# Attention into balanced experts: loads paced six in front instead of three, x held in pieces and written behind all loads, the gate's norms taken sooner

## The chip, the cores and the metric

One core of a Trainium2 chip runs the whole program. The metric is the device time of one execution in microseconds; lower is better. The kernel before takes 627.1 us, the median of three runs (626.71 to 636.63).

The core has five engines with queues of their own: TensorE (PE; its weight loads are listed as PEld), VectorE (DVE), ScalarE (ACT), GpSimd (POOL) and SyncE (SP), which here does little else than issue transfers. An engine works through its queue in order, and an instruction that waits holds up all that stands behind it.

## The reference

```
kv  = einsum('bhsd,bhse->bhde', k, v)          # 8 batches, 8 heads, 576 rows, 64 columns
out = einsum('bhsd,bhde->bhse', q, kv)
x   = out / sqrt(mean(out*out, -1) + 1e-6) * g_norm   # then (b, h, s, d) -> (b*s, h*d) = 4608 x 512

logits = x @ w_gate                            # 4608 x 8
order  = argsort(-logits.flatten())            # greedy: the largest logit first,
                                               # an expert takes 576 tokens and is then full
for e in range(8):
    y[mask_e] = relu(x[mask_e] @ w1[e]) @ w2[e]
```

There is no softmax: attention is two matrix products and a norm over each head. Which token goes to which expert depends on all logits at once, so the choice can begin only when the last batch's logits are there.

## The kernel before

The program has two parts. The first, attention, is written by hand for TensorE, VectorE, ScalarE and SyncE: on these engines the order in the queue is the order in the code. It fills the logits (lg) and writes the normed rows x to DRAM (x_dram). The second chooses the tokens of one expert after another, gathers their rows out of x_dram with indirect transfers of GpSimd (L793), and runs the experts' two layers on TensorE. Its code is untouched by the change.

**Loads.** k, v and q of a batch come in two halves each, six transfers of 576 KB (load, L83). They are all issued by SyncE, in the order k, v, q, k, v, q, each through paced (L75). The loads of batches 0 and 1 stand at the head of the program, those of batch b+2 at the end of prepare(b) (L401), which runs in pieces inside the work of batch b-1. Each of k, v and q has two buffers, so a load of batch b+2 also waits until TensorE has read batch b. paced adds a wait: from the seventh transfer on, a transfer is issued when the third in front of it in the list has landed. The writes of x go through paced too and are in the same list.

**One batch.** prepare(b) sums k times v over the rows into kv_ps (sum_kv, L341, four pairs of heads, each of 72 or 36 listed matmuls with its neighbour), turns q in five groups (turn_q, L326, against the identity matrix ident), and makes kvx, the right side of the second product: kv itself and, beside it, kv times the gate's weights (gw), so that the second product yields the row and its gate logits at once. work(b) then does four or five tiles of 128 rows (tiles, L410): the product into o_ps (L433), squares on ScalarE, their sum on VectorE, a copy into o_sb. At a batch's end come the norm (inv), the logits (L465), and the scaled rows xo: on GpSimd (L470) for batches 0 to 6, on ScalarE (L475) for the last one. The pieces of prepare(b+1) are slipped between the tiles of work(b), so on TensorE sums and turns of one batch alternate with the products of the batch before.

**Writes of x.** tiles appends to a list of writes, one for each two tiles (512 KB, or 256 KB for a fifth tile alone). At the end of a batch's work, L520 issues writes from the front of the list as long as eight or more wait, and all in the last batch. So the first three writes are issued at the end of the work of batch 3, between the loads of batches 6 and 7. One tile xo of five buffers holds the scaled rows of a batch until they are written.

**The start.** While the first loads come, TensorE runs filler products (ones, L265). The gate's weights and g_norm are loaded by ScalarE's queue (L100, L105). gate_norms (L272) multiplies them, squares and sums them on VectorE, and sums over the partitions on TensorE (L278); from this gate_bound makes the limits between which the later search for thresholds runs. VectorE makes ident out of two iotas (L111 to L117).

## Time and profile before

| | |
|---|---|
| three runs | 627.1, 636.63, 626.71 us |
| the profiled execution | 627.37 us, its span 625.6 us |
| PE busy | 585.3 us, 94% of the span |
| DVE, ACT, POOL busy | 373.3, 179.3, 412.3 us |
| mean granted clock of TensorE | 0.967 |
| read and written in DRAM | 71.32 MB, 18.87 MB |
| loads of k, v, q | 48 of 576 KB |
| writes of x | 16 of 512 KB, 4 of 256 KB |
| first product of batch 7 | 108.73 us |
| gather of the first expert's tokens | from 137.49 us |

The profile is of one execution, whose own time stands in the table; its span runs from the first to the last instruction. Times in its views count from the span's start. The attention lies between 0 and about 118 us; the first choice of tokens, a chain of short steps, between there and 137 us; the experts' layers after that. In the rows, "<-" names what ended a wait, "issue" stands where the profile shows nothing that was waited for, and "x72" is a count of instructions. The clock is the share of full speed that TensorE was granted.

### The profile page before, as it was taken

Reading aid. Unit: us, or ns where it says so; the run is one execution under the profiler, and the core shown is the slowest. Engines: PE = TensorE matmul, PEld = TensorE weight load, DVE = VectorE, ACT = ScalarE, POOL = GpSimd, SP = SyncE. Lnnn points to the kernel's source line nnn. Section 1 sums busy time; section 2 is a strip of 40 time slices with the busy share of each in tenths; the row PEclk is TensorE's granted clock in tenths of the full one; section 3 lists DMA queues with packets and bytes.
Section 4 is the critical chain, followed back from the end, with each engine's and each line's share of the span. In section 5 each row is a group of like instructions: output and inputs, shape, how many; then the busy total and the mean of one; then the engine's idle time right before and its main releaser. Section 6 shows DMA issues by size and latency. Waiting matters only on the chain.

```text
span 625.6 us, 12011 instructions
## 1 busy us (share of the span) xinstructions
PE 585.3 (94%) x4644; PEld 460.5 (74%) x4644; DVE 373.3 (60%) x1172; ACT 179.3 (29%) x387; POOL 412.3 (66%) x367
## 2 busy tenths in 40 slices
PE   7998888459999999999999999999999999999993
PEld 4887777336788678777867886788678877867881
DVE  2676764868878796778728763885481255024320
ACT  1565654814221222022212221221123123213200
POOL 0154434216999989696869668966987796966603
PEclk9999997759999999999999999999999999999997
DMA  8998899748045280092056106503633062010002
GB/s 286 314 312 275 283 305 341 271 137 260 0 143 203 75 318 27 2 344 76 1 178 204 40 16 226 180 1 100 223 98 135 2 210 77 1 51 25 1 2 80
DMA packets 41410, 91.07 MB, mean 146 GB/s; under 512 B 3456, under 2 KB 3456, under 8 KB 41344
## 3 DMA queue, kind: packets, MB, share of 16 engines
q1 hardware_dynamic: 34752, 71.31, 33.5%
q0 software_dynamic: 5888, 18.88, 9.2%
q8 instruction: 39, 0.64, 0.4%
q14 instruction: 27, 0.22, 0.1%
q10 hardware_dynamic: 704, 0.02, 0.1%
HBM read 71.32 MB, written 18.87 MB: 144 GB/s over the span
## 4 chain that ended last, share of the span: by engine, by line
PE 76%; DMA 13%; DVE 5%; issue 2%; POOL 2%; ACT 1%; POOLq 0%; DVEq 0%; ACTq 0%
PE h_ps L966 33%; PE y_ps L1066 31%; DMA v_sb<-in_v_dram 11%; PE y_ps L1080 4%; PE t_ps L874 3%; PE o_ps L433 2%; PE kv_ps L345 1%; DMA q_sb<-in_q_dram 1%; PE given_ps L580 1%; DMA g_col<-in_g_norm_dram 1%; PE given_ps L576 1%; PE qt_ps L330 1%; DVE ms L447 1%; DMA xg<-x_dram,ids 1%; POOL out_dram L883 1%
## 5 line engine op out<-in xcount | busy, mean ns | idle before, releaser
L966 PE MATMUL h_ps<-xt,w_sb 128*128 128x288 f32 x384 | 101.0, 412 | 0.9 <-ACT xt L877 0.8
L978 ACT ACTIVATE hid<-hid 128x288 f32<-128x288 f32 x128 | 55.6, 443 | 147.5 <-DVE hid L961 139.4
L966 PEld LDWEIGHTS h_ps<-xt,w_sb 128*128 128x128 f32 x384 | 70.8, 190 | 24.8 <-issue 5.7
L961 DVE TENSOR_TENSOR hid<-h_ps,u 128x288 f32<-128x288 f32 x128 | 56.8, 454 | 28.9 <-PE h_ps L966 24.6
L966 PE MATMUL h_ps<-sx,sw 128*128 128x288 f32 x256 | 67.9, 407 | 0.1
L793 POOL DMA_INDIRECT xg<-x_dram,ids x40 | 38.2, 955 | 34.9 <-DVE upper L633 22.6
L1066 PE MATMUL y_ps<-tw,sh 128*128 128x256 f32 x256 | 61.1, 383 | 0.0
L1066 PE MATMUL y_ps<-tw,hid 128*128 128x256 f32 x256 | 60.9, 381 | 0.0
L1066 PE MATMUL y_ps<-w_sb,hid 128*128 128x256 f32 x256 | 59.5, 382 | 0.0
L966 PEld LDWEIGHTS h_ps<-sx,sw 128*128 128x128 f32 x256 | 48.4, 190 | 13.9 <-DVE u L961 0.6
L877 ACT ACTIVATE xt<-t_ps,g_col 128x512 f32<-128x512 f32 (+1 forms) x40 | 25.8, 644 | 110.3 <-PE t_ps L874 110.3
L1066 PEld LDWEIGHTS y_ps<-w_sb,hid 128*128 128x128 f32 x256 | 47.4, 190 | 6.4
L1066 PEld LDWEIGHTS y_ps<-tw,sh 128*128 128x128 f32 x256 | 47.3, 190 | 6.1
L1066 PEld LDWEIGHTS y_ps<-tw,hid 128*128 128x128 f32 x256 | 47.1, 190 | 6.0
L470 POOL TENSOR_TENSOR xo<-o_sb,inv 128x512 f32<-128x512 f32 x31 | 32.5, 1077 | 27.7 <-ACT sq L439 11.1
L961 DVE TENSOR_TENSOR y_sb<-y_ps,u 128x512 f32<-128x512 f32 x24 | 16.5, 689 | 53.5 <-PE y_ps L1066 53.5
L961 DVE TENSOR_TENSOR u<-h_ps,u 128x288 f32<-128x288 f32 x96 | 41.9, 449 | 10.3 <-PE h_ps L966 8.3
L433 PE MATMUL o_ps<-kvx,qt 64*128 64x72 f32 (+1 forms) x640 | 41.3, 274 | 4.5 <-DVE kvx L396 2.7
L433 PEld LDWEIGHTS o_ps<-kvx,qt 64*128 64x128 f32 (+1 forms) x640 | 36.3, 182 | 9.1 <-issue 7.8
L896 POOL TENSOR_TENSOR sh<-hid 128x512 f32<-128x512 f32 x16 | 20.3, 1268 | 33.0 <-ACT hid L978 31.9
L896 POOL TENSOR_TENSOR tw<-w_sb 128x512 f32<-128x512 f32 x32 | 40.0, 1272 | 0.2
L883 POOL DMA_INDIRECT out_dram<-y_sb,outs x32 | 31.3, 977 | 11.5 <-issue 10.2
(214 smaller groups left out, 1064.2 us busy)
## 6 DMA issues: line engine op xcount, KB each, us to landing
w_sb<-in_moe_w_dram SPq DMA_DIRECT2D x16, 1024.0 KB, 6.2
w_sb<-in_moe_w_dram SPq DMA_DIRECT2D x8, 2048.0 KB, 14.1
k_sb<-in_k_dram SPq DMA_DIRECT2D x16, 576.0 KB, 5.8
v_sb<-in_v_dram SPq DMA_DIRECT2D x16, 576.0 KB, 6.0
q_sb<-in_q_dram SPq DMA_DIRECT2D x16, 576.0 KB, 6.1
x_dram<-xo SPq DMA_DIRECT2D x16, 512.0 KB, 4.3
x_dram<-xo SPq DMA_DIRECT2D x4, 256.0 KB, 4.7
xg<-x_dram,ids POOLq DMA_INDIRECT x40
```

Of the source, the lines that this page charges most:

```text
L433: nc.tensor.matmul(o_ps[rows_at, rp, (2 * r2 + l) * W:(2 * r2 + l + 1) * W], lhsT=turned_q[bn][ks, l, block // 2:block // 2 + m].rearrange ...
L470: nc.gpsimd.tensor_tensor(xo[:, t], o_sb[:, t, :, 0:D], inv[:, t * H:(t + 1) * H].rearrange("p (h o) -> p h o", o=1).to_broadcast([P, H, D ...
L793: tokens = nc.gpsimd.indirect_dma_start(out=xg[0:nr], out_offset=None, in_=x_dram, in_offset=bass.IndirectOffsetOnAxis(ap=ids[0:nr, n:n + ...
L874: nc.tensor.transpose(t_ps[:, d, 0:nr], xg[0:nr, d * P:(d + 1) * P], ident[0:nr, 0:nr])
L877: nc.scalar.mul(xt[:, :, a:a + nr], t_ps[:, :, 0:nr], g_col)
L883: put = nc.gpsimd.indirect_dma_start(out=out, out_offset=bass.IndirectOffsetOnAxis(ap=ids_of[t][0:nr, n:n + 1], axis=0), in_=y_sb[0:nr, :] ...
L896: in_order(nc.gpsimd.tensor_tensor(o, x, y, op=op))
L961: nc.vector.tensor_tensor(o, p_ps, u, op=AL.add)
L966: nc.tensor.matmul(o, lhsT=left[:, d, f * P:(f + 1) * P], rhs=right[:, d], start=d == 0, stop=d == KH - 1)
L978: nc.scalar.activation(h, h, ACT.Relu)
L1066: nc.tensor.matmul(p_ps[:, n], lhsT=left[:, f, n * P:(n + 1) * P], rhs=right[:, f], start=(f == 0), stop=(f == FH - 1))
L1080: nc.tensor.matmul(y_ps[l * nr:(l + 1) * nr], lhsT=hid[:, l * FH + f, a:a + nr], rhs=w2[:, l * FH + f, :], start=(f == 0), stop=(f == FH - 1))
```

## The change

Four edits in the attention part.

- paced: the wait is for the sixth transfer in front, not the third. It still begins with the seventh transfer.
- The scaled rows are held in pieces of two tiles (12 buffers) or one tile (4 buffers) in place of one tile for a whole batch in five buffers. No write is issued before the end of the work of batch 4, where the list holds twelve; the later ones go at the end of each batch's work. Since the loads of batch 7 are issued within the work of batch 4, all writes stand behind all loads.
- odd, kv, kvt and part have one buffer in place of two.
- gate_norms is called ahead of turn_q(0) and turn_q(1) in prepare(0).

```diff
     loaded = {}
-    AHEAD = 3
+    AHEAD = 6
     issued = []
     def paced(dma):
-        if len(issued) >= 2 * AHEAD:
+        if len(issued) >= AHEAD:
             tc.add_manual_dep(dma.ins, issued[-AHEAD].name,
...
             ones(3)
+            gate_norms()
             turn_q(0)
             turn_q(1)
-            gate_norms()
             ones(4)
...
-        odd = att.tile([D, 2, NP * D], FT, name="odd", tag="odd")
+        odd = att.tile([D, 2, NP * D], FT, name="odd", tag="odd", bufs=1)
...
-        xo = att.tile([P, T, H, D], FT, name="xo", tag="xo", bufs=LAG + 1)
+        xo = [att.tile([P, min(2, T - x), H, D], FT, name="xo", tag=f"xo{min(2, T - x)}", bufs=(4, 12)[min(1, T - x - 1)])
+              for x in range(0, T, 2)]
...
-                nc.gpsimd.tensor_tensor(xo[:, t], o_sb[:, t, :, 0:D],
+                nc.gpsimd.tensor_tensor(xo[t // 2][:, t % 2], o_sb[:, t, :, 0:D],
...
-                xo[:, x:y].rearrange("p t h d -> p t (h d)"))))
+                xo[x // 2].rearrange("p t h d -> p t (h d)"))))
...
-            while len(writes) >= 2 * LAG or b + 1 == B and writes:
+            while b + 4 >= B and writes:
                 writes.pop(0)()
```

kv, kvt and part get bufs=1 in the same way as odd. Three places show how the change moves instructions. SyncE's queue, from the loads of the second half of batch 6 to the first writes, before the change:

```order
L89 DMA q_sb<-in_q_dram 128x2x576
L479 DMA x_dram<-xo 128x2x512 x3
L89 DMA k_sb<-in_k_dram 128x2x576
L89 DMA v_sb<-in_v_dram 128x2x576
L89 DMA q_sb<-in_q_dram 128x2x576
```

and after it, from the second half of batch 7 on:

```order
L89 DMA k_sb<-in_k_dram 128x2x576
L89 DMA v_sb<-in_v_dram 128x2x576
L89 DMA q_sb<-in_q_dram 128x2x576
L479 DMA x_dram<-xo 128x2x512 x4
L479 DMA x_dram<-xo 128x512
L479 DMA x_dram<-xo 128x2x512 x4
```

The three writes that stood between two batches' loads have moved behind the last load.

VectorE's queue at the head of the program, the difference (+ is after, - is before). gone and who are cleared there, row_f is the iota as a number, and qt is the first copy of turned q:

```order
 L214 MEMSET gone 128x36
 L216 MEMSET who 128x36
+L274 TENSOR_SCALAR gw<-gw,g_col 128x64
+L276 TENSOR_TENSOR gsq<-gw 128x64
+L277 TENSOR_REDUCE g_146<-gsq 128x8
 L111 CAST iota_p<-iota_p_i 128x1
 L115 CAST row_f<-row_i 128x128
@@ -29,7 +32,4 @@
 L174 TENSOR_SCALAR know<-iota_p 128x1
 L334 COPY qt<-qt_ps 128x2x256
-L274 TENSOR_SCALAR gw<-gw,g_col 128x64
-L276 TENSOR_TENSOR gsq<-gw 128x64
-L277 TENSOR_REDUCE g_146<-gsq 128x8
```

The three steps on the gate's weights have moved not only ahead of the copy of q but ahead of the two casts from which ident is made.

TensorE's queue at the same place; begun_ps is the target of the fillers and of the gate's sum:

```order
 L268 LDWEIGHTS ones_b
 L268 MATMUL begun_ps<-wide,ones_b 128x512
+L278 MATMUL begun_ps<-g_146,ones_f 128x8
 L330 MATMUL qt_ps<-ident,q_sb 128x128 x8
-L278 MATMUL begun_ps<-g_146,ones_f 128x8
 L268 LDWEIGHTS ones_b
```

The gate's sum has moved ahead of the eight turns of q.

## The prediction

> **What bounds the kernel now.** I read the page first: the span, the clock line, and the chain that ended last.

> ```profile
> span 625.6 us, 12011 instructions
> PEclk9999997759999999999999999999999999999997
> DMA  8998899748045280092056106503633062010002
> PE 76%; DMA 13%; DVE 5%; issue 2%; POOL 2%; ACT 1%; POOLq 0%; DVEq 0%; ACTq 0%
> ```

> The expert layers (from about 146 us on) are PE's own. The DMA share of the chain lies in the first six or seven slices, the attention, and that is where the change lies. So the second view is that stretch cut into pieces of equal work: each row below runs over two batches, from the first o_ps product of batch 1, 3, 5 to that of batch 3, 5, 7. Columns are microseconds, busy time of each engine with its instruction count, granted clock, DMA share, GB/s.

> ```profile
> 30.29:53.21 22.92, 21.91 (x525) 19.13 (x525) 17.02 (x43) 15.12 (x32) 11.87 (x13) 1.00 0.95 310
> 53.21:78.77 25.56, 22.13 (x525) 19.20 (x525) 17.14 (x45) 14.98 (x31) 11.88 (x13) 1.00 0.87 274
> 78.77:108.73 29.96, 26.07 (x525) 22.63 (x525) 17.60 (x44) 15.30 (x32) 11.83 (x13) 0.83 0.93 321
> ```

> The same 525 matmuls take 22.92, then 25.56, then 29.96 us. The first pair is what PE can do when fed: 21.91 of 22.92 us busy. The others are 2.64 and 7.04 us longer, 9.68 us together. That is all that attention can give back without doing less work. What it is made of, the waits of PE between 14 and 109 us show (total, times, longest):

> ```profile
> PE kv_ps L345 <- DMA v_sb<-in_v_dram: 3.0, 3, 1.2
> PE o_ps L433 <- DVE kvx L396: 2.7, 6, 0.8
> PE o_ps L433 <- issue: 1.5, 1, 1.5
> PE qt_ps L330 <- DMA q_sb<-in_q_dram: 0.9, 2, 0.7
> PE qt_ps L330 <- issue: 0.4, 1, 0.4
> ```

> Late loads: 3.0 + 0.9 = 3.9 us. Waits with no releaser ("issue"): 1.5 + 0.4 = 1.9 us. The kvx waits are in the undisturbed pair too, and stay. The remaining 9.68 - 3.9 - 1.9 = 3.9 us is the clock: the third pair has 0.83, and its PE busy time is 26.07 - 21.91 = 4.2 us above the first's, which agrees. The timeline says where these fall.

> ```profile
> 90.33 0.47 PE L433 MATMUL o_ps<-kvx,qt 64*64 64x72 f32 x12 [1.51 <-issue]
> 92.48 1.74 PE L433 MATMUL o_ps<-kvx,qt 64*128 64x72 f32 x16 [0.31 <-DVE kvx L396]
> 95.29 1.33 PE L345 MATMUL kv_ps<-v_sb,k_sb 64*64 64x64 f32 x36 [1.06 <-DMA v_sb<-in_v_dram]
> 97.27 1.09 PE L330 MATMUL qt_ps<-ident,q_sb 128*128 128x128 f32 x4 [0.66 <-DMA q_sb<-in_q_dram]
> ```

> and, in windows of 1 us (columns as above):

> ```profile
> 92.00:93.00 1.00, 0.69 (x10) 0.55 (x9) 0.34 (x2) 1.00 (x4) 0.00 (x0) 0.89 0.91 286
> 93.00:94.00 1.00, 1.00 (x12) 1.00 (x10) 0.75 (x3) 0.08 (x1) 0.00 (x0) 0.50 0.82 187
> ```

> The clock halves late in the 92-93 window, in the middle of a thin stretch: 1.51 us idle before 90.33, 1.06 before 95.29, 0.66 before 97.27.

> **The change part by part.** *Pacing and order of the loads.* Before, a load waits until the third in front has landed, and three writes of x stand between the loads of batches 6 and 7:

> ```profile
> 16.00:81.00 65.00, 59.91 (x1383) 51.76 (x1381) 46.01 (x130) 40.25 (x81) 26.36 (x31) 1.00 0.91 299
> 80.13 0.37 SPq L89 DMA_DIRECT2D q_sb<-in_q_dram  x1
> 81.65 5.23 SPq L479 DMA_DIRECT2D x_dram<-xo  x3
> 87.93 0.37 SPq L89 DMA_DIRECT2D k_sb<-in_k_dram  x1
> k_sb<-in_k_dram SPq DMA_DIRECT2D x16, 576.0 KB, 5.8
> ```

> A batch is six loads of 576 KB, 3.54 MB. An undisturbed batch of PE work lasts 22.92/2 = 11.46 us, so the loads keep up from 309 GB/s on. The queue gave 299 GB/s at a DMA share of 0.91, just short of it, and then lost 87.93 - 80.13 = 7.8 us to three writes where a load is otherwise issued every 2 us. With six in flight the 16 engines have work while one load's last pieces straggle in. I take the share to go to about 1.0: 299/0.91 = 329 GB/s (my estimate from that row). From 309 GB/s up, the 3.9 us of load waits go. The low end is 299 GB/s unchanged, worked out under the rivals. What is late next is PE itself, with its kvx waits.

> Buffers do not stop this: the loads of batch b+2 may go once PE has summed and turned batch b. Undisturbed, that is 11.46 us and more before batch b+2's first product, against six loads at 329 GB/s = 10.8 us, and batch 1's loads need no buffer freed at all.

> *The clock.* Without the gaps at 95.29 and 97.27 I take the clock to stay at 1.00, as it does from 30 to 79 us with 0.4 to 1.2 us waits: 3.9 us gained. The bound on the other side is that it falls all the same: 0.

> *The "issue" waits.* Nothing in the change is aimed at them; I keep 1.9 us. Were they loads in disguise, 1.9 us more would go; were they instruction fetches, they could grow (a rival).

> *The writes.* All 20 now stand behind the last load. What waits for them is the gather of the first expert's tokens:

> ```profile
> 121.91 6.06 SPq L479 DMA_DIRECT2D x_dram<-xo  x3
> DMA to landing us min/median/max: 2.8/4.5/6.2
> 137.49 1.16 POOL L793 DMA_INDIRECT xg<-x_dram,ids  x1 [22.62 <-DVE upper L633]
> ```

> The last write is issued at 127.97 and lands some 4.5 us later, 5 us ahead of the gather, which waits for DVE. The last three writes come out of ScalarE's scaling, which moves with PE, so this distance stays if the queue is clear. 16 x 512 KB + 4 x 256 KB = 9.4 MB at 299 GB/s is 32 us; behind loads that end between 88 us (28.3 MB at 329 GB/s from about 3 us on) and 98 us (at 299) that is 120 to 130 us, against a gather at about 137.5 - 7.3 = 130.2. Cost 0; if that cover went, its price is at most a few us. The queue holds no weights before these writes. The pieces of x (12 and 4 buffers) hold batches 0 to 5 without any write; batch 6's first pieces need only writes 1 and 2. One buffer in place of two for odd, kv, kvt and part: each was last read some 10 us before it is written again. Cost 0, hidden by the batch between.

> *The gate's norms.* The order shows that VectorE's three steps now stand ahead of the casts that make ident, and TensorE's L278 ahead of the turns of q. VectorE waits there for the gate weights, whose queue (q10) moves its last packets here:

> ```profile
> q10 hardware_dynamic: 2, 0.00, 0.7%
> 2.16 0.11 DVE L111 CAST iota_p<-iota_p_i 128x1 f32<-128x1 int32 x1
> 2.44 0.28 DVE L117 TENSOR_SCALAR ident<-row_f,iota_p 128x128 f32<-128x128 f32 x1
> 12.45 0.25 DVE L274 TENSOR_SCALAR gw<-gw,g_col 128x64 f32<-128x64 f32 x1
> 12.99 0.27 DVE L277 TENSOR_REDUCE g<-gsq 128x8 f32<-128x64 f32 x1
> 10.66 1.14 PE L330 MATMUL qt_ps<-ident,q_sb 128*128 128x128 f32 x8
> 13.31 0.39 PE L278 MATMUL begun_ps<-g,ones_f 128*128 128x8 f32 x2 [1.51 <-DVE g L277]
> 13.56 1.02 PE L268 MATMUL begun_ps<-wide,ones_b 128*128 128x512 bf16 x4
> 14.51 1.38 PE L345 MATMUL kv_ps<-v_sb,k_sb 64*64 64x64 f32 x72
> ```

> (The q10 row is of the window 11.4 to 11.6 us.) So the gate weights are there at about 11.5. The three steps take 12.99 + 0.27 - 12.45 = 0.81 us, and from the cast to the end of ident it is 2.72 - 2.16 = 0.56 us: ident at 12.9 instead of 2.7. The eight turns take 1.14 us, to 14.0; then the four fillers, 14.51 - 13.56 = 0.95 us: the second half of batch 0's sum begins at 15.0 instead of 14.51. The old 1.51 us wait of PE goes, but a longer one, from 10.7 to 12.4, comes before the turns: 0.5 us lost. Bounds: 0 if the gate weights come 0.5 us sooner, 1.5 if they come 1 us later since the seventh load is now issued before 11.1 us and shares the engines with them.

> *Sum.* Loads -3.9, clock -3.9, norms +0.5, the rest 0: -7.3 us. The profiled execution took 627.37 us, 1.8 more than its span and 0.3 above the median of the runs shown (627.1), so I work from it: 627.4 - 7.3 = **620.1 us**. The rows from 108.73 us on (end of attention, first choice of tokens, experts) should only move.

> **The rivals.** *A: depth brings no speed.* The loads stay at 299 GB/s; only the three writes are out of the way. For it: in the first pair of batches 310 GB/s came with three in flight. The engines are full from 3 us on (first row, the load queue in the window of 3 to 4 us), so 48 loads, 28.3 MB, last to 3 + 94.7 = 98 us. The last k and v land about 1.5 us before that. From the second half of a sum to the first o_ps that follows, batch 1 takes 30.29 - 24.12 = 6.2 us (second row, and the first pair's start).

> ```profile
> q1 hardware_dynamic: 160, 0.36, 101.1%
> 24.12 1.47 PE L345 MATMUL kv_ps<-v_sb,k_sb 64*64 64x64 f32 x72
> ```

> That gives 102.7 instead of 108.73: 6.0 us, **621.4 us**; the norms' 0.5 us and the issue waits hide behind the loads. [...]

> *B: the clock falls all the same.* The fall at 92.9 us came before the waits that the change removes, after the 1.51 us issue wait, which I keep. Then the 3.9 us stay: **624.0 us**. [...]

> *C: slower, PE starved of instructions.* Between 14 and 113 us the instruction queue moved 16 blocks through the same engines as the loads:

> ```profile
> q1 hardware_dynamic: 14067, 29.79, 89.9%
> q8 instruction: 16, 0.26, 1.1%
> ```

> The 1.51 us issue wait may be such a block held up. If a queue twice as deep makes each block late, every 0.46 us per block (7.3/16) eats the whole gain; from there on the kernel is slower. At 1.5 us for each, 16 x 1.5 - 1.9 = 22 us more: **642 us**. Against it: 14 of 16 came unnoticed at a 0.9 share. [...]

> *D: more than I say.* The issue waits go as well: 627.4 - 9.7 + 0.5 = **618.2 us**.

> *E: the change doesn't do what it says.* If something else than the loosened wait holds the issues back, no more than three are in flight, and this is A in time.

> **How the numbers follow.** Forecast 0.50; A and E together 0.17; B 0.13; D 0.12; C 0.05 (0.03 of it beyond 2%); 0.03 for a late gather or a slow start. The time is the forecast's. From 616.5 (D with a somewhat shorter tail) to 626 (B with the norms at 1.5 us and a late write) about 85% lies by these, and I leave it there, since the causes can add up. A change of 2%, 12.5 us, is about what a measurement of this kernel can tell from none; the whole of the recoverable time is 9.7 us. So faster by over 2% has 0.05, slower by over 2% 0.03, within 2% 0.92.

> **What would show it.** Right: batch pairs of about 23 us three times over, no wait for v_sb or q_sb after 20 us, clock 1.00 until the tail, loads all issued before 90 us at a DMA share near 1.0, batch 0's second sum at about 15.0, gather near 130. A shows as waits for v_sb late in the attention at about 300 GB/s; B as a 0.5 clock before 100 us without load waits; C as many "issue" waits of PE. It would be wrong altogether if the gather then waited for a write, or if the expert layers, which I only shift, changed their length.

## The result, and the profile after

The changed kernel takes 632.97 us (median of 8 runs, 630.52 to 640.86), the kernel before 627.04 us (8 runs beside them, 622.84 to 636.63). The ratio is 1.0101, with a 95% interval of 1.006 to 1.0142: about 1% slower, less than 2% but clearly not nothing, where 620.1 us was forecast. (Medians are of all executions; the ratios leave out those that lie over 1.5% above the fastest of their kernel.) The profiled execution took 633.65 us.

The page of the changed kernel, lines as shown of before:

```profile
span 631.9 us, 12008 instructions
PEclk9996996858999999999999999999999999999997
DMA  8987899327218163074045205601643062011002
PE 85%; DVE 7%; issue 3%; DMA 2%; ACT 1%; POOL 1%; POOLq 0%; ACTq 0%; DVEq 0%
```

DMA has left the chain that ended last (13% to 2%), as the change meant it to. But the clock line, which before had one dent (slices 7 to 9), now has one more in the fourth slice. A short fall at the head, from 13.79 to 17.20 us, shows only in the finer windows further down.

The same three pieces of equal work, from the first o_ps product of batch 1, 3, 5 to that of batch 3, 5, 7 (microseconds, busy time with instruction count of PE, PEld, DVE, ACT, POOL, then granted clock, DMA share, GB/s):

```profile
34.14:62.12 27.98, 26.61 (x524) 23.16 (x525) 17.22 (x43) 15.11 (x32) 11.88 (x13) 0.82 0.78 264
62.12:86.11 23.99, 22.03 (x525) 19.21 (x525) 17.38 (x45) 15.18 (x32) 11.90 (x13) 1.00 0.87 286
86.11:114.90 28.79, 26.70 (x524) 23.24 (x525) 17.37 (x44) 15.17 (x32) 11.89 (x13) 0.82 0.94 341
```

Before they took 22.92, 25.56 and 29.96 us. The first pair, which had been undisturbed, is now 5.06 us longer, and 4.70 of these are PE's own busy time (26.61 for 21.91) at a clock of 0.82. The second and third are 1.57 and 1.17 us shorter. The first o_ps of batch 1 comes at 34.14 instead of 30.29, 3.85 us later: 2.66 us of it come from a later second half of batch 0's sum and 1.10 us from the first wait shown below. From the last row on all only shifts: 28.70 us from 114.90 to the gather at 143.60 (28.76 before), 488.3 us from there to the end (488.1). The sum is 3.85 + 5.06 - 1.57 - 1.17 - 0.06 = 6.1 us at the gather; the two executions differ by 6.3.

What PE waited for between 19 and 115 us (total, times, longest):

```profile
PE o_ps L433 <- DVE kvx L396: 2.4, 6, 0.7
PE o_ps L433 <- issue: 1.8, 1, 1.8
PE kv_ps L345 <- issue: 1.5, 2, 1.1
PE qt_ps L330 <- issue: 1.1, 1, 1.1
PE kv_ps L384 <- DVE kv L370: 0.2, 1, 0.2
```

No wait for v_sb or q_sb is left. The waits with no releaser have grown from 1.9 to 1.8 + 1.5 + 1.1 = 4.4 us. The timeline of PE says where three of the four are (start, duration, work, in brackets the idle time before):

```profile
28.61 0.91 PE L345 MATMUL kv_ps<-v_sb,k_sb 64*64 64x64 f32 x39 [1.10 <-issue]
79.81 0.38 PE L330 MATMUL qt_ps<-ident,q_sb 128*128 128x128 f32 x2 [1.14 <-issue]
97.89 0.47 PE L433 MATMUL o_ps<-kvx,qt 64*64 64x72 f32 x12 [1.78 <-issue]
```

Each stands in the middle of a group of like products, and the profile names nothing that it waited for: 39 of the 72 products of a sum, two of four turns, 12 of 32 products. I take the instructions themselves to be missing; the trace shows of them only the packets of the instruction queue. In the first, the last 16 KB packet of the instruction queue ahead of it started at 25.99 and took 1.09 us; the wait ended 1.5 us behind it; in the other two the distance to the end of such a packet is 1.6 and 1.2 us.

### The profile page after: what moved, and what is told of

Same layout as the page of the kernel before. It is cut to its first block, busy times and chain, and to the rows that moved or that the text cites. A ratio compares the mean times of both kernels' runs of the same rounds, so it can differ in the third digit from the quotient of the medians.

```text
span 631.9 us, 12008 instructions
## 1 busy us (share of the span) xinstructions
PE 592.3 (94%) x4644; PEld 466.0 (74%) x4644; DVE 374.0 (59%) x1172; ACT 179.5 (28%) x387; POOL 412.8 (65%) x367
## 4 chain that ended last, share of the span: by engine, by line
PE 85%; DVE 7%; issue 3%; DMA 2%; ACT 1%; POOL 1%; POOLq 0%; ACTq 0%; DVEq 0%
PE h_ps L966 34%; PE y_ps L1066 30%; PE o_ps L433 5%; PE y_ps L1080 4%; PE kv_ps L345 4%; PE t_ps L874 3%; PE qt_ps L330 3%; DMA gw<-in_moe_w_gate_dram 1%; DVE ms L447 1%; PE given_ps L580 1%; PE given_ps L576 1%; DMA xg<-x_dram,ids 1%; POOL out_dram L883 1%; DVE kv L370 0%; DVE pick L243 0%
## 5 line engine op out<-in xcount | busy, mean ns | idle before, releaser
L793 POOL DMA_INDIRECT xg<-x_dram,ids x40 | 38.2, 954 | 34.9 <-DVE upper L633 22.6
L433 PE MATMUL o_ps<-kvx,qt 64*128 64x72 f32 (+1 forms) x640 | 43.0, 282 | 4.3 <-DVE kvx L396 2.4
L433 PEld LDWEIGHTS o_ps<-kvx,qt 64*128 64x128 f32 (+1 forms) x640 | 38.0, 189 | 9.2 <-issue 7.8
L376 POOL COPY kvx<-kv 64x512 f32<-64x512 f32 x16 | 9.8, 610 | 48.3 <-DVE kv L370 47.8
## 6 DMA issues: line engine op xcount, KB each, us to landing
k_sb<-in_k_dram SPq DMA_DIRECT2D x16, 576.0 KB, 6.4
v_sb<-in_v_dram SPq DMA_DIRECT2D x16, 576.0 KB, 7.1
q_sb<-in_q_dram SPq DMA_DIRECT2D x16, 576.0 KB, 7.9
```

Source lines behind the costliest of these rows:

```text
L433: nc.tensor.matmul(o_ps[rows_at, rp, (2 * r2 + l) * W:(2 * r2 + l + 1) * W], lhsT=turned_q[bn][ks, l, block // 2:block // 2 + m].rearrange ...
L793: tokens = nc.gpsimd.indirect_dma_start(out=xg[0:nr], out_offset=None, in_=x_dram, in_offset=bass.IndirectOffsetOnAxis(ap=ids[0:nr, n:n + ...
```

## The experiments

The kernel before was timed on the same chip beside each; ratios are to it, with 95% intervals.

### Each part by itself

Kernel norms_back is the changed kernel with the norms at their old place:

```diff
             ones(3)
-            gate_norms()
             turn_q(0)
             turn_q(1)
+            gate_norms()
```

> The changed kernel with the gate's norms put back behind the first two turns of q; all else as changed. Theory N (the order at the head costs): the second half of batch 0's sum begins at 14.5 us instead of 17.2, no half clock before 20 us, and the time falls by 2.7 us, from 633.0 to about 630.3. Rival (the depth of the queue alone made it slower, the head was made up for later): 633 as changed. By neither does it come below 627 unless the clock falls of the later batches, which the theory on thin windows (C) takes for a matter of where the windows of 3.41 us lie, happen to miss.

Measured: 630.4 us, 1.0085 [1.0046, 1.0124]. The second half of batch 0's sum begins at 14.60 us, and the median is the one that theory N names. But the ratio falls only from 1.0101 to 1.0085, which the two intervals do not tell from no gain. The rest of the change makes the kernel slower by itself.

Kernel norms_only is the kernel before with this one edit the other way, gate_norms ahead of the turns.

> The kernel before with only the gate's norms taken sooner. Theory N: the head is 2.7 us later, as in the changed kernel. What of it reaches the end depends on the loads: where TensorE waits for them anyway (3.9 us in all in the profile of before) a later start costs nothing. So between 627.0 (all absorbed) and 629.7 (none). Rival (no loss at the head without the deeper queue, since the gate's weights then come sooner): second half of batch 0's sum by 15.0 us and 627.0.

Measured: 629.11 us, 1.0064 [1.0026, 1.0102], within theory N's time. Set beside norms_back, single costs seem not to add up to the whole (1.0064 and 1.0085 against 1.0101), but the intervals are too wide to show it. PE's timeline at the head of norms_only:

```profile
12.82 0.39 PE L278 MATMUL begun_ps<-g,ones_f 128*128 128x8 f32 x2 [1.83 <-DVE iota_p L111]
13.33 1.16 PE L330 MATMUL qt_ps<-ident,q_sb 128*128 128x128 f32 x8
14.28 1.91 PE L268 MATMUL begun_ps<-wide,ones_b 128*128 128x512 bf16 x4
16.12 2.06 PE L345 MATMUL kv_ps<-v_sb,k_sb 64*64 64x64 f32 x72
```

The turns run at full speed (1.16 us), the four fillers behind them at half (1.91 for 0.95), and so does the sum (2.06 for 1.38): it begins 1.6 us later than before, and is longer.

Kernel depth_only is the kernel before with the wait alone:

```diff
-    AHEAD = 3
+    AHEAD = 6
...
-        if len(issued) >= 2 * AHEAD:
+        if len(issued) >= AHEAD:
```

> The kernel before with only the pacing loosened (the sixth transfer in front, not the third); the three writes stay between the loads, norms as before. Theory I-depth (a deeper load queue makes TensorE's instruction blocks later): waits without releaser of 4 to 6 us in the attention, load waits near 0 but for the three writes, time 3 to 5 us over the kernel before, as the changed kernel with the norms put back (ratio 1.004 to 1.009). Rival (depth is harmless, the loss lies in holding all writes back): ratio 0.99 to 1.00.

Measured: 634.28 us, 1.0100 [1.0061, 1.0139]. The deeper queue alone costs as much as the whole change, a little more than the 1.004 to 1.009 expected. Its profile had 4.4 us of waits with no releaser, within the 4 to 6 us expected, and no wait for a load.

Kernel writes_behind is norms_back with the pacing of before (AHEAD 3, from the seventh transfer on). What is left of the change is the writes behind the loads, the pieces of x and the single buffers.

> The changed kernel with the norms put back and the pacing of before (third in front); what is left of the change is x in pieces, written behind all loads, and the single buffers. Theory I-depth: as the kernel before or better, since three writes are out of the loads' way: ratio 0.990 to 1.000, waits without releaser about 2 us. Rival (load traffic without a gap makes the blocks late at any depth): waits without releaser of 4 us and more, load waits gone, ratio 1.003 to 1.009, as with depth six.

Measured: 626.51 us, 0.9999 [0.9956, 1.0042]. These parts cost nothing and bring nothing that an interval of 0.4% either way would show. Its waits of PE with no releaser were 0.8 + 0.8 + 0.7 = 2.3 us, and it had no wait for a load although only three were in flight.

### Without the loads

Kernel no_loads is norms_back without the loads of batches 2 to 7: their sums and turns use the data of batches 0 and 1 again, so that all other work stays as it is.

```diff
+        if b >= 2:
+            loaded[name, b] = kept[name, b % 2]
+            return
```

> The changed kernel with the norms put back, and without the loads of batches 2 to 7: they use the k, v and q of batches 0 and 1, so the output is that of other inputs. Theory I (a block of instructions comes late because it shares the engines of the transfers with the loads): the waits of TensorE without releaser in the attention (4.4 us in the changed kernel) go to 0. Rival (TensorE runs through its instructions faster than they can be fetched, whatever the loads do): they stay at 4 us or grow. Both expect no wait for loads after 20 us and about 11.5 us for a batch.

Measured: one execution, 616.9 us. The three pairs of batches, and all waits of PE between 15 and 100 us:

```profile
30.38:52.98 22.60, 21.62 (x525) 19.00 (x526) 17.03 (x43) 15.13 (x32) 11.88 (x13) 1.00 0.29 108
52.98:75.65 22.67, 21.61 (x525) 18.97 (x525) 17.29 (x45) 15.11 (x32) 11.89 (x13) 1.00 0.29 107
75.65:98.25 22.60, 21.61 (x525) 18.97 (x525) 17.22 (x44) 15.12 (x32) 11.88 (x13) 1.00 0.29 108
```

```profile
PE o_ps L436 <- DVE kvx L399: 3.3, 7, 0.7
PE kv_ps L387 <- DVE kv L373: 0.2, 1, 0.2
```

Every wait with no releaser is gone (norms_back, the same kernel with the loads, had 4.9 us in its profile) and the clock stays at 1.00 over all three pairs, though the blocks of instructions still have to come (13 of them between 20 and 90 us; 10 in the profile of norms_back). So these waits come with the traffic of the loads; this rests on one execution, but no other profile of this study is without such waits. That it is the instructions that are late stays my reading of it. The time of a block's packet itself does not show it. In the trace of the changed kernel, between 14 and 119 us:

```profile
q8 instruction: 16, 0.26, 1.0%
```

That is 1.0% of 16 engines over 105 us for 16 blocks, 1.05 us a block; before it was 1.1% of 99 us, 1.09 us. If a block comes late, the time is lost before its packet starts or after it ends, and the trace shows neither.

### Fillers where PE's work is thin

The clock seemed to fall behind the ends of the batches' preparation, where PE has a run of small products, waits for kvx, and often has a wait with no releaser (rows in the section on why the prediction was wrong). Kernel fill_ends is norms_back with filler products there, three for an even batch, one for an odd one:

```diff
             t_ps = psa.tile([P, 4, P], FT, name="qt_ps", tag="tr", bufs=2)
+            for _ in range((3, 1)[b % 2] if n == 4 and b > 0 else 0):
+                nc.tensor.matmul(t_ps.rearrange("p x c -> p (x c)"), lhsT=ones_b, rhs=wide, start=True, stop=True)
```

> The changed kernel with the norms put back and filler products (128x512 bf16, three after an even batch's preparation, one after an odd one's, batches 1 to 7) where TensorE waits for kvx at a batch's end. Theory C (the clock halves for 10.24 us after a 3.41 us window with too little work, and the thin stretch is the end of an even batch): no half clock between 20 us and the tail; each fall spared is worth 4.7 us, so 621 to 626 us against 630 for the same kernel without fillers. Rival 1 (the falls come from the waits without releaser, not from thin work): the falls stay where those waits are, 630. Rival 2 (fillers only lengthen TensorE's path): up to 7 x 0.4 us more, 633.

Measured: 627.24 us, 1.0039 [1.0006, 1.0073]; 13 products more, of 0.27 us each (three took 0.81 us in the trace), and the kernel is faster than norms_back, not slower. But theory C named 621 to 626 us and no half clock between 20 us and the tail, and missed both. In the profiles of fill_ends and of its repeat below, the clock fell at 90.31 and 90.09 us, for 6.8 us each time, during a wait with no releaser, as rival 1 said of the place. In fill_ends this was

```profile
91.10 0.99 PE L435 MATMUL o_ps<-kvx,qt 64*64 64x72 f32 x21 [2.16 <-issue]
```

The fillers of that batch stand behind this wait, at 93.90 us. So fillers help, and do not keep the clock up by themselves. Kernel before_fill is the kernel before with the same fillers.

> The kernel before with the filler products at the batches' ends (three after an even batch's preparation, one after an odd one's), nothing else. Theory C (thin windows halve the clock): the fall in the attention goes in most executions, 0.5 to 1% faster than before (ratio 0.990 to 0.996); fillers in the changed kernel took 1.0085 to 1.0039. Rival (fillers help only where instructions come late): 1.000.

Measured: 623.16 us, 0.9957 [0.992, 0.9994], within theory C's range; its profile has no fall of the clock between 20 us and the tail, and its longest wait with no releaser is 1.3 us.

Kernel before_again is the kernel before once more, to see how far one profile can be trusted.

> The kernel before once more, for a second profile at a depth of three. If the waits without releaser hang on depth, they are again about 2 us in the attention, with load waits of about 4 us; if an execution trades one for the other, their sum is about 6 us and the shares differ.

Measured: 632.47 us in this execution, at a clock of 0.954. It had no wait of PE for a load at all, 3.9 us of waits with no releaser (1.9 in the profile that I predicted from), and 20.5 us of half clock from 77.5 us on, with 6.8 us more at the head, where that profile had 10.2 in the attention. Both forms of the expectation (about 2 and 4 us, or 6 us in sum) are missed. One execution's length is no measure; but it says that one profile of this kernel is a sample.

### How deep, and what of it is clock

Kernel depth4 is norms_back with AHEAD = 4.

> The changed kernel with the norms at their old place and a depth of four; depth three gave 0.9999 and depth six 1.0085. Theory T with a gradual cost (each further load in flight adds to the wait of an instruction block): about a third of the way, 1.002 to 1.005, issue waits of PE between 3 and 5 us. Rival S (a step, the blocks are late as soon as the queue never runs dry): 1.006 to 1.010, as at six. Rival P (only the place where a block falls beside the loads decides, depth is by chance): anywhere, also below 1.000.

Measured: 629.01 us, 1.0015 [0.997, 1.0061], with 4.9 us of waits with no releaser in its profile. With three in flight it was 0.9999 and with six 1.0085. The middle lies just below T's 1.002 to 1.005; a gradual cost (T) and chance (P) both lie within the interval, and of the step's range (S) only its lower edge, 1.006, does. The waits are as long as at six, though, so this run does not show that they grow with each load in flight.

Kernel fill_depth3 is fill_ends with the pacing of before; fill_ends_again is fill_ends unchanged.

> The changed kernel with the norms at their old place, the depth of three and the filler products at the ends of the batches' preparation; beside the run with fillers and depth six (1.0039) only the depth differs. Theory T (a deeper queue of loads makes PE's instruction blocks late, some 4.8 us of waits for 3.2, and the thin stretch behind then lets the clock fall): with fillers the clock stays, so what is left of the depth is the waits alone: ratio to before 0.994 to 0.999, 1.6 us or more below the filled kernel of depth six, and below before. Rival K (the depth costs only through the clock, its waits are as long at both depths): the same as fill_ends_again within 0.25%. Rival W (writes behind the loads cost something that the fillers lay bare): above 1.000.

> The changed kernel with the norms at their old place, depth six and the filler products, once more, on the chip of the two runs beside it. Theory T: 1.002 to 1.006 as before (1.0039 [1.0006, 1.0073]), PE's issue waits 4.4 us or more, and above the filled kernel of depth three by 0.25% or more. Rival K: the same as the filled kernel of depth three within 0.25%.

Measured: fill_depth3 623.36 us, 0.9958 [0.9917, 1.0]; fill_ends_again 627.28 us, 1.0004 [0.9965, 1.0042]. The two differ by the depth alone, on one chip; taking the runs of both again and again at random, their means have the ratio 0.995 [0.992, 0.998]. So the depth costs 0.5% with fillers too, and K's "the same within 0.25%" is a miss. So is T's 1.002 to 1.006 for fill_ends_again, though its interval reaches it. Waits of PE in the attention, fill_depth3 first:

```profile
PE kv_ps L347 <- issue: 3.5, 4, 1.8
PE o_ps L435 <- issue: 0.4, 1, 0.4
PE kv_ps L396 <- issue: 0.2, 1, 0.2
```

```profile
PE o_ps L435 <- issue: 2.2, 1, 2.2
PE kv_ps L347 <- issue: 1.8, 2, 1.1
PE kv_ps L396 <- issue: 1.2, 2, 1.0
PE qt_ps L332 <- issue: 0.6, 1, 0.6
PE qt_ps L330 <- issue: 0.2, 1, 0.2
```

That is 4.1 us at a depth of three and 6.0 at six. The waits with no releaser were, in us, at three 1.9, 4.5, 2.3, 3.6, 4.1 (before, norms_only, writes_behind, before_fill, fill_depth3; mean 3.3), and at six 4.4, 5.5, 6.0 (the changed kernel, fill_ends, fill_ends_again; mean 5.3). before_again, at three, had 3.9, and depth_only and norms_back, at six, 4.4 and 4.9. The groups overlap, and each number is one execution. One place shows the difference at the same instruction: the wait ahead of the last 39 products in the middle of batch 1's sum. At six it was 1.10, 1.40 and 1.12 us, and 1.20 in both other profiles; at three it was absent three times (before, writes_behind, fill_depth3), and 0.46, 0.62 and 1.13 us in the other three; at four it was absent. What the load queue did around that place, from 20 to 34 us, in fill_depth3 and in fill_ends_again:

```profile
20.00:34.00 14.00, 13.69 (x317) 11.79 (x313) 10.65 (x42) 9.06 (x19) 1.71 (x3) 1.00 0.92 300
```

```profile
20.00:34.00 14.00, 12.78 (x299) 11.09 (x299) 10.56 (x37) 8.62 (x17) 2.34 (x3) 1.00 1.05 388
```

300 GB/s at a share of 0.92 against 388 at 1.05, and PE is 0.9 us less busy beside the fuller queue: 1.12 us of its idle time there are this one wait.

Single profiles differ too much to say what part is clock, but every run lists its span and mean granted clock. In the windows of 3.41 us of the two kernels' profiles the clock has only the levels 1.00 and 0.50; taking that for every run, 2 x (1 - clock) x span is the time at half clock, and the span less half of that is what would be left without it, if all of it were lost time. Means of the runs that the ratios go by, in us:

| kernel | depth | runs | time | at half clock | span less half of that |
|---|---|---|---|---|---|
| before (all three chips' runs) | 3 | 70 | 625.9 | 41.1 | 603.6 |
| changed | 6 | 7 | 633.1 | 48.9 | 606.9 |
| norms_only | 3 | 12 | 629.5 | 47.5 | 604.0 |
| depth_only | 6 | 7 | 631.3 | 48.2 | 605.4 |
| norms_back | 6 | 11 | 631.2 | 48.1 | 605.4 |
| depth4 | 4 | 9 | 627.6 | 41.6 | 605.0 |
| writes_behind | 3 | 8 | 624.3 | 39.6 | 602.7 |
| fill_ends | 6 | 12 | 627.4 | 42.0 | 604.6 |
| fill_ends_again | 6 | 12 | 627.1 | 41.6 | 604.5 |
| fill_depth3 | 3 | 12 | 624.0 | 35.8 | 604.3 |
| before_fill | 3 | 10 | 623.3 | 32.0 | 605.5 |

The one profile of no_loads, whose clock stayed at 1.00 up to 106 us, gives 30.8 us at half clock by this reckoning, so about that much of each row lies behind the attention. The standard errors are 0.6 to 1.0 us for the time, 1.4 to 2.8 us for the half clock and 0.3 to 0.8 us for the last column; for before, with its 70 runs, they are 0.3, 0.9 and 0.2 us. Of the 7.2 us between before and changed, 3.9 are half clock (7.8 us more of it) and 3.3 are not. Within a kernel one more us at half clock goes with 0.33 us more span, not 0.5; by that the clock is 2.5 us of the 7.2. For norms_only (6.4 us more at half clock) the clock is 3.2 of its 3.6 us by the first reckoning and 2.1 by the second. Between fill_depth3 and fill_ends_again (5.8 us more) it is 2.9 of 3.1 us by the first and 1.9 by the second. T's premise that with fillers the clock stays was wrong: fillers shortened the half-clock time at both depths, and six still had more of it. Whether what the depth costs there is clock or waits (4.1 us against 6.0 in the two profiles) is not settled.

fill_depth3 and before_fill, at 0.996, are the best versions of the study. Both are 0.4% below before, at the edge of what the intervals tell from nothing.

## Why the prediction was wrong, step by step

**Loads (-3.9): the waits went as said, the rate did not, and the size stood on one execution.** Every wait for v_sb and q_sb after 19 us is gone, and the loads are all issued before 88 us, as forecast. From 20 to 34 us, before and then after:

```profile
20.00:34.00 14.00, 13.68 (x332) 11.99 (x333) 11.25 (x40) 8.86 (x18) 3.09 (x4) 1.00 0.94 316
```

```profile
20.00:34.00 14.00, 12.61 (x272) 10.73 (x272) 9.72 (x37) 7.72 (x16) 2.40 (x4) 1.00 1.05 382
```

382 GB/s, more than the 329 that I had estimated: rival A, that depth brings no speed, is refuted for this stretch, and so is E. Over the stretch from which I had worked, 16 to 81 us, the rate is another (first row; then two loads that follow each other in SyncE's queue):

```profile
16.00:81.00 65.00, 60.25 (x1326) 51.11 (x1328) 41.58 (x114) 35.16 (x70) 24.93 (x28) 0.91 0.89 305
47.42 0.47 SPq L89 DMA_DIRECT2D q_sb<-in_q_dram  x1
56.93 0.37 SPq L89 DMA_DIRECT2D k_sb<-in_k_dram  x1
```

305 GB/s against 299 before, at a share of 0.89 where I had taken 1.0. "Buffers do not stop this" was wrong: loads now run ahead until both buffers are full and then wait for PE, 48 us in all, 9.0 us of them between the two rows. They come in bursts, and the longest of these waits, the 9.0 us from 47.89 us on, lies beside the half clock from 47.92 to 58.16 us; in the last window of that, from 54.76 us on, the DMA share is 0.16, where it is 1.05 from 20 to 34 us. What speed there is does not help PE in the first stretch either: its busy time falls from 13.68 to 12.61 us, and the first wait with no releaser, 1.10 us, lies there. And the 3.9 us were a property of the profiled execution of before: norms_only, writes_behind, fill_depth3 and before_again had no such wait with three in flight, and before_fill had 1.8 us. There was less to gain than one profile showed.

**The "issue" waits (kept at 1.9): the step that failed.** I put them at no change, with the depth of the queue as a rival, C, at a chance of 0.05. They became 4.4 us, and at six in flight they were 4.4 to 6.0 us in all five profiles, at three 1.9 to 4.5 in six. That such waits come with the loads, as rival C has it, no_loads shows in kind (no loads, no such wait), at a much smaller size than its 642 us: four waits, not sixteen. That the depth is what makes the kernel slower is shown by depth_only (1.0100) and by writes_behind against norms_back (0.9999 and 1.0085); that it does so through these waits is argued from the profiles. My argument against it, that 14 of 16 blocks came unnoticed at a share of 0.9, was taken from the very state that the change removes. In no_loads the waits are gone with the traffic, while a block's own packet takes 1.05 us beside the deeper queue and took 1.09 us before. Where the delay arises the trace does not show.

**The clock (-3.9): wrong in sign.** I tied the fall to the gaps that late loads make, though both gaps lay behind it, and let it go with them; rival B said that it would stay. It stayed, and a second one came in the attention and a third at the head: 23.9 us at half clock up to 110 us for 10.2 before. The windows around the three (columns as above), with one in which it did not fall:

```profile
10.38:13.79 3.41, 0.92 (x5) 0.44 (x4) 1.45 (x10) 0.00 (x0) 0.00 (x0) 1.00 1.06 384
13.79:17.20 3.41, 3.41 (x16) 1.96 (x15) 1.90 (x10) 0.59 (x1) 0.00 (x0) 0.50 1.06 393
44.52:47.93 3.41, 2.73 (x42) 2.30 (x38) 2.90 (x10) 2.16 (x5) 0.12 (x1) 1.00 0.89 244
47.93:51.34 3.41, 3.41 (x51) 2.93 (x52) 1.89 (x4) 1.71 (x3) 3.17 (x3) 0.50 0.96 338
71.82:75.24 3.42, 2.91 (x52) 2.48 (x46) 2.77 (x10) 2.21 (x5) 0.20 (x1) 1.00 0.91 268
95.72:99.13 3.41, 1.63 (x50) 1.37 (x43) 1.75 (x6) 1.01 (x4) 0.58 (x1) 1.00 1.04 396
99.13:102.54 3.41, 3.41 (x42) 2.95 (x44) 2.25 (x7) 1.86 (x5) 0.34 (x1) 0.50 1.06 406
```

Before each fall lies a window of 3.41 us in which PE did little, though it was never idle throughout: 0.92, 2.73 and 1.63 us busy, with 5, 42 and 50 products. In the window that ends at 75.24 it was 2.91 us with 52, and the clock stayed. Busy time alone does not decide. Two windows of the kernel before, of which only the second was followed by a fall:

```profile
58.66:62.07 3.41, 2.21 (x90) 2.00 (x86) 1.56 (x4) 1.22 (x3) 0.63 (x1) 1.00 0.88 291
89.38:92.79 3.41, 2.15 (x40) 1.84 (x40) 1.58 (x5) 1.90 (x5) 0.00 (x0) 1.00 0.84 275
```

PE was busy about as long in both, but behind 90 products the clock stayed and behind 40 it fell; the exact measure stays open. The end of an even batch's preparation (small products into kvx's other half, turns, the wait for kvx) lies in the windows of the changed kernel that end at 47.93, 75.24 and 99.13, with 2.73, 2.91 and 1.63 us of busy PE; that its place in the window decides whether the clock falls is my reading, and no run moves it alone. A wait with no releaser of 1.78 us, as before 97.89, lies in the third window too. Such waits and the falls go together in all twelve profiles with loads: of 13 falls between 20 us and the end of the attention, 12 have a wait with no releaser, of 0.8 to 2.2 us, that reaches into the window of 3.41 us ahead, and of the 11 such waits of 1.5 us or more 10 stand before a fall in this way. The one fall without is that at 47.92. So I should not have counted on the clock: by this reading a shift of PE's work can put a thin stretch into a window, and more waits make more of them. That the waits raise the odds agrees with the table's half-clock times, 48 to 49 us at six against 40 and 41 at three (writes_behind, before), and 42 against 36 with fillers; norms_only has 47.5 at three, with a fall at the head and one at 72.26 us in its profile. That a given wait caused a given fall is argued, not shown.

**The norms (+0.5): right in kind, too small.** Measured at the second half of batch 0's sum: 17.17 instead of 14.51, +2.66 us, where I had 15.0 and at most 1.5 us of loss. VectorE, then PE:

```profile
12.27 0.25 DVE L274 TENSOR_SCALAR gw<-gw,g_col 128x64 f32<-128x64 f32 x1 [10.02 <-DMA v_sb<-in_v_dram]
13.00 0.14 DVE L111 CAST iota_p<-iota_p_i 128x1 f32<-128x1 int32 x1
13.32 0.28 DVE L117 TENSOR_SCALAR ident<-row_f,iota_p 128x128 f32<-128x128 f32 x1
```

```profile
13.14 0.39 PE L278 MATMUL begun_ps<-g,ones_f 128*128 128x8 f32 x2 [2.37 <-DVE iota_p L111]
13.65 1.88 PE L330 MATMUL qt_ps<-ident,q_sb 128*128 128x128 f32 x8
15.33 1.91 PE L268 MATMUL begun_ps<-wide,ones_b 128*128 128x512 bf16 x4
17.17 1.03 PE L345 MATMUL kv_ps<-v_sb,k_sb 64*64 64x64 f32 x54
```

The weights let VectorE go at 12.27, not at 11.5 (the row names v_sb, but the step reads only gw and g_col), and ident is done at 13.60, not 12.9: 0.7 us, within my bounds. The casts behind L274 in the queue ran at 13.00, where they ran at 2.16 before. The rest is the clock again. PE's longer wait, 2.37 us, lies in the window to 13.79, of which PE is busy for 0.92 us; the clock is 0.50 from there to 17.20, and the turns and fillers run from 13.65 to 17.17, 3.52 us instead of 1.14 + 0.95. I had priced the wait and not a fall of the clock behind it. The edit alone costs 0.6% (norms_only), while taking it out of the changed kernel gains 0.2% (norms_back). Later windows may fall otherwise once the head has shifted, but the two figures also agree within their intervals.

**Writes, buffers, tail (0): right.** The end of SyncE's loads, and the gather:

```profile
87.27 0.86 SPq L89 DMA_DIRECT2D q_sb<-in_q_dram  x1
88.23 3.40 SPq L479 DMA_DIRECT2D x_dram<-xo  x3
```

```profile
143.60 1.16 POOL L793 DMA_INDIRECT xg<-x_dram,ids  x1 [22.64 <-DVE upper L633]
```

The first write stands behind the last load, the gather waits for VectorE and not for a write, and writes_behind at 0.9999 prices these parts together at nothing, within 0.4%.

**The range.** It reached to 626 because I let all causes of both traces be bounded by what the profile of before still had to give; nothing in it but the norms' 0.5 to 1.5 us was a loss. The terms that I now take the change to add (more waits with no releaser, more thin windows) had their only place in a rival with a price of 15 us and a chance of 0.05. A small size of the same, a few us with the clock behind it, had no place, and that is what came.

What stays open: what PE waits for beside a full queue (the trace names no releaser), whether the waits cause the falls of the clock, and how the 7.2 us divide between waits and clock more closely than 2.5 to 3.9 us of clock.

## What to carry to other kernels

A deeper transfer queue was not free here: 382 GB/s for 316 came with 1% more time, and the waits of PE with no releaser, 4.9 us in the profile of norms_back, were gone in that of no_loads. Time the shallower depths too, for three in flight was faster than six (0.9999 and 1.0085, with fillers 0.9958 and 1.0004) though some of its executions waited for loads. The load rate ended here where the buffers were full (48 us of waits for PE, 305 GB/s from 16 to 81 us): look for waits of the queue on its consumer. Before pricing a gap, look at the clock behind it: a thin stretch of some 3 us was followed by 3.4 to 10.2 us of half speed in most of these profiles (41 us in that of depth_only), and a few filler products there brought 0.4% where the reordering of the loads brought nothing. Profile the kernel before twice ahead of a forecast whose terms are as small as 4 us, since the load waits here were 3.9 us in one profile of the same kernel and none in the next.

## What was not expected of the hardware

The other surprise is that more work was less time: the kernel before with filler products has 32.0 us at half clock for 41.1, and takes 2.6 us less in all.
